# Moving each segment's four output stores from GpSimd's queue to SP's, one at each of four places in the next segment

## The chip, the cores and the metric

The kernel runs on one core of one Trainium2 chip. The core has five engines that work side by side, each through its own list of instructions in order: TensorE (PE, matrix multiplies, with the loading of weights shown apart as PEld), VectorE (DVE), ScalarE (ACT), GpSimd (POOL) and SyncE (SP), which does nothing but issue transfers. Transfers between the DRAM and the on-chip memory run on 16 DMA engines; SP, ScalarE and GpSimd can issue them. The metric is the time of one execution on the device in microseconds (us), lower being better.

## The reference

The function has two independent parts, whose results stand side by side in the last dimension of the output (1 x 2048 x 1280). Part A is a dilated sliding-window attention of 32 heads. Part B is the one that matters here: a recurrent attention with a small memory. It walks through the 2048 rows of x in 64 segments of 32 rows, and each segment needs the memory that the segment before it has made:

```python
mem = mem0                                     # 8 x 640
for s in range(64):
    xs = x[:, s * 32:(s + 1) * 32, :]
    h = jnp.concatenate([mem, xs], axis=1)     # 40 rows
    q = jnp.einsum('btd,dhe->bhte', h, Wq)     # 32 heads of 192
    k = jnp.einsum('btd,dhe->bhte', h, Wk)
    v = jnp.einsum('btd,dhe->bhte', h, Wv)
    scores = jnp.einsum('bhqe,bhke->bhqk', q, k) * scale
    scores = jnp.where(mask[None, None], scores, -1000000000.0)
    p = _softmax(scores, axis=-1)
    o = jnp.einsum('bhqk,bhke->bhqe', p, v)
    o = jnp.einsum('bhte,hed->btd', o, Wo)
    mem = o[:, :8, :]                          # memory of the next segment
    outs.append(o[:, 8:, :])                   # 32 rows of the output
```

Wq, Wk and Wv are 640 x 6144 each and Wo is 6144 x 640, all in bf16: together more than the on-chip memory holds.

## The kernel before

Part A runs first. Part B begins while it ends, some 150 us into the execution, and goes on to the end.

**Weights.** They are cut into units: a unit of q, k or v is 128 x 1536 elements (384 KB), named by its matrix, its head group g (four groups of eight heads) and one of five slices of the 640 inputs; a unit of o is 128 x 1280 (320 KB), 24 of them. Most units lie in the on-chip memory throughout (tiles named wres_q, wres_k, wres_v, wres_o). The others are streamed: in every segment 8 units of k, 10 of v and 5 of o are read again from copies in the DRAM (wcopy_k, wcopy_v, wcopy_o). All units of q are resident. Streamed units land in a pool of seven buffers (tiles named t). `get_unit(u)` gives the resident tile or calls `fetch(u)`, whose L474 issues the transfer on SP. Such a transfer has to wait until TensorE has finished with the unit that stood in the same buffer, seven fetches earlier.

**One segment.** Its work is a list of tokens, written out by hand in `ORDER` (`FIRST` for segment 0), and `step` carries out one token after another. For each head group g: `q.g`, `k.g`, `v.g` project (L561 in `project32`), `e.` tokens copy the results out (ScalarE or VectorE, L567 and L600), `T.` tokens transpose them in VectorE (L571), `S.g` makes the scores (L625), `sb`, `mx`, `sub`, `send` are the softmax, `tp`, `PT` and `mix` apply it to the values (L664, L688), `ot` keeps the result (L696 to L698). `out.g.h` projects the first three groups' results by Wo (L713), `last` the fourth's (L739). `close` (L743 to L751) ends the segment: it adds the parts, writes the new memory rows into HX, from which the next segment's projections read (L747), and writes all 32 rows into the tile XS (L748). XS holds four blocks of 160 columns one under the other, 32 partitions each, and the four stores of L750 write 24 rows of each block to the output. XS is also the tile into which `load_x` (L534, at the token `ve.2`) brings the x rows of the next segment, and from which `turn_x` (L530, at the token `tx`) transposes them into HX.

TensorE takes 32 rows at a time, so a segment's own projections hold the 8 memory rows and the first 24 rows of x. The last 8 rows of x take a path of their own, since their projections need no memory: they are made for four segments together, for a different part of the head groups in every segment, kept in small tiles (Lb, L591) and copied into place by GpSimd (L586, L607). The result for these rows goes to the DRAM by way of the tile OL and the transfer late_o (L697, L698, both on GpSimd) and is projected by Wo after the last segment (`project_late`).

**What sets the order.** The instructions of TensorE, VectorE, ScalarE and SP stand in the order in which the code calls them. So a fetch stands on SP where `get_unit` is called for its unit, and SP comes to it as soon as all issues before it have gone out; SP is ahead of TensorE by up to the seven buffers. GpSimd's instructions are placed by the scheduler.

The order of the tokens around the change, of segments 1 to 63:

```python
ORDER = """
    q.0 e.q0 T.q0 k.0 k.1 e.k0 T.k0 q.1 S.0 sb.0 e.k1 e.q1 mx.0 sub.0 v.0 T.q1 ve.0 T.k1 q.2 S.1 send.0
    e.q2 T.q2 sb.1 mx.1 k.2 tp.0 v.1 e.k2 q.3 PT.0 sub.1 mix.0 T.k2 send.1 tp.1 S.2 ve.1 ot.0 sb.2 e.q3
    PT.1 mx.2 sub.2 k.3 T.q3 send.2 out.0.0 e.k3 v.2 out.0.1 mix.1 T.k3 S.3 ot.1 tp.2 sb.3 mx.3 v.3 PT.2
    ve.2 mix.2 sub.3 out.1.0 send.3 out.1.1 ot.2 tp.3 ve.3 out.2.0 out.2.1 part tx PT.3 mix.3 ot.3 last
    join ql close eql Tql
"""
```

The streamed units of a segment go out in this order: k0 (2), k1 (2), v0 (3), k2 (2), v1 (2), k3 (2), v2 (3), v3 (2), then the load of XS, then o (5).

Of the kernel before, what the change touches and what calls it, by code (L numbers as in the profile page):

```python
# [23 lines left out]
def part_a(ctx, tc, A_x, A_wqkv, A_wo, out, ident, emit_loads):  # L24
# [241 lines left out]
    with tc.manual_schedule(engines={mybir.EngineType.PE, mybir.EngineType.DVE, mybir.EngineType.Activation}):  # L266
        pq = ps_q.tile([128, BIG], FP32, tag="q")
        for _ in range(LEAD_IN):
            nc.tensor.matmul(pq[:, 0:8], lhsT=ident, rhs=ident[:, 0:8], start=True, stop=True)
# [35 lines left out]
EVACUATE = {"k0": "SV", "k1": "SS", "k2": "VS", "k3": "SS", "q0": "VV", "q1": "SS", "q2": "SS", "q3": "VV"}  # L305
HEADS = ("VS", "SV", "VS", "SV")
SPREAD = "SSVV"
LEAD_IN = 114
HEAD = 10

# [8 lines left out]
def part_b(ctx, tc, B_x, B_mem0, B_Wq, B_Wk, B_Wv, B_Wo, out, ident, n_seg, pre, nbuf, mid):  # L319
    nc = tc.nc  # L320
    Dm, H, Dh, M, SEG, L = 640, 32, 192, 8, 32, 40
# [3 lines left out]
    out2 = out.rearrange("b s d -> (b s) d")  # L325
# [203 lines left out]
    def turn32(dst, src):  # L529
        nc.vector.transpose(dst, src.rearrange("p (f k) -> p k f", k=5))  # L530
# [39 lines left out]
    def turn_in_place(t):  # L570
        nc.vector.transpose(t, t)  # L571

    def columns_of(m, n0, n1):
        t = KT[:] if m == "k" else QT[:, 0:12 * L].rearrange("p (f n) -> p f n", n=L)
        return t[:, :, n0:n1]
# [19 lines left out]
    def project_qk(s, m, g):  # L595
        return project32([ahead, main] if renewed(s, m, g) else [main], m, g)

    def evacuate(m, ps, copies):
        sb = to_sb(ps[0], copies[0]) if len(ps) > 1 else None
        copies[1](columns_of(m, 0, 32), ps[-1][:].rearrange("p (f n) -> p f n", n=32))  # L600
        return sb

    def fill_late(s, m, g, sb):
        if sb is not None:
            return turn_late(sb, m, g, s, s)
        b = late.pop((m, g, s))
        nc.gpsimd.tensor_copy(columns_of(m, 32, L), b[:])  # L607
        free.append(b)

    def values(s, g):  # L610
        return project32([ahead, main] if renewed(s, "v", g) else [main], "v", g)

    def keep_values(g, ps):
        S_(Vst[:], ps[-1][:])  # L614
        if len(ps) > 1:
            S_(LV[g][:], ps[0][:])

    def scores(g):
        Sps = bank()[:, 0:4 * L].rearrange("p (a n) -> p a n", n=L)
        for outer in range(2):  # L620
            for a in range(4):
                for h in range(2):
                    k0, k1, c = (0, 128, 2 * h) if outer else (64 * h, 64 * h + 64, 1)
                    f = 3 * a + c
                    nc.tensor.matmul(Sps[64 * h:64 * h + 64, a, :], lhsT=QT[k0:k1, L * f:L * f + 64], rhs=KT[k0:k1, f, :],  # L625
                                     start=(outer == 0 and a == 0), stop=(outer == 1 and a == 3),
                                     tile_position=(k0, 64 * h))
        return Sps

    def soft_begin(Sps):  # L630
        nc.vector.scalar_tensor_tensor(out=Sps, in0=Sps, scalar=scale,  # L631
                                       in1=mask[:].unsqueeze(1).to_broadcast([128, 4, L]),
                                       op0=ALU.mult, op1=ALU.add)
        return Sps

    def soft_max(t1):
        mx = small.tile([128, 4], FP32, tag="mx")
        nc.vector.tensor_reduce(out=mx[:], in_=t1[:], axis=AX.X, op=ALU.max)  # L638
        return mx

    def soft_exp(t1, mx):
        nc.vector.tensor_tensor(t1[:], t1[:], mx[:].unsqueeze(2).to_broadcast([128, 4, L]), op=ALU.subtract)
        nc.scalar.activation(t1[:], t1[:], ACTF.Exp)

    def soft_end(s, g, t1):
        sm = small.tile([128, 4], FP32, tag="mx")
        nc.vector.tensor_reduce(out=sm[:], in_=t1[:], axis=AX.X, op=ALU.add)
        nc.vector.reciprocal(sm[:], sm[:])
        put_p(s, g, t1, sm)
# [18 lines left out]
    def spread_p(g, pt):  # L668
        PT = one.tile([128, 4, 2, L], BF16, tag="PT")
        if SPREAD[g] == "S":  # L670
            for b in range(2):
# [71 lines left out]
    def close(s, Y, part, partT):  # L743
        Ysb, T = XS[:], Vst[:, 0:320].bitcast(FP32).rearrange("p (k n) -> p k n", n=SEG)
        if s + 1 < n_seg:
            turn32(T, Y)
            nc.vector.tensor_tensor(HX[:, 0, :, 0:M], T[:, :, 0:M], partT[:, :, 0:M], op=ALU.add)  # L747
        nc.vector.tensor_tensor(Ysb, Y, part, op=ALU.add)  # L748
        for j in range(4):
            nc.gpsimd.dma_start(out2[SEG * s:SEG * s + SEG - M, Dm + 160 * j:Dm + 160 * j + 160],  # L750
                                Ysb[32 * j + M:32 * j + SEG])  # L751

    def segment(s):
        last = s + 1 == n_seg
        engine = {"S": S_, "V": V_}
        got = {}

        def project(m, g):
            if m == "v":
                got["v", g] = values(s, g)  # L760
            else:
                got[m, g] = project_qk(s, m, g)
                if last and (m, g) == ("k", 3):
                    load_late((2, 3))

        def step(name, *at):
            g = int(at[0][-1]) if at else None
            if name in "qkv":
                project(name, g)
            elif name == "e":  # L770
                m = at[0][0]
                got["sb", m, g] = evacuate(m, got.pop((m, g)), [engine[c] for c in EVACUATE[at[0]]])
            elif name == "T":
                m = at[0][0]
                keep = fill_late(s, m, g, got.pop(("sb", m, g)))
                turn_in_place(columns_of(m, 0, 32))
                if m + at[0][1] == "k0" and s and keep:
                    got["keep"] = keep
                elif keep:
                    keep()  # L780
                if at[0] == "k1" and "keep" in got:
                    got.pop("keep")()
            elif name == "S":
                got["S", g] = scores(g)
            elif name == "sb":
                got["t", g] = soft_begin(got.pop(("S", g)))
            elif name == "mx":
                got["mx", g] = soft_max(got["t", g])
            elif name == "sub":
                soft_exp(got["t", g], got.pop(("mx", g)))  # L790
            elif name == "send":
                soft_end(s, g, got.pop(("t", g)))
            elif name == "tp":
                got["p", g] = turn_p(g)
            elif name == "PT":
                got["PT", g] = spread_p(g, got.pop(("p", g)))
            elif name == "ve":
                keep_values(g, got.pop(("v", g)))
                if g == 2:
                    load_x(s + 1)  # L800
                elif last and g == 1:
                    load_late((0, 1))
            elif name == "mix":
                got["mix", g] = mix(g, got.pop(("PT", g)))
            elif name == "ot":
                keep_mix(s, g, got.pop(("mix", g)), [engine[c] for c in HEADS[g]])
            elif name == "out":
                g, half = int(at[0]), int(at[1])
                if "Y" not in got:
                    got["Y"] = ps_y.tile([128, 320], FP32, tag="y", name="Y")  # L810
                project_out(got["Y"], g, range(4 * half, 4 + 2 * half))
            elif name == "part":
                got["part"] = join_begin(got["Y"])
            elif name == "join":
                join_end(got["Y"], got["part"])
                got["partT"] = None if last else turn_part(got["part"])
            elif name == "tx":
                turn_x(s + 1)
            elif name == "ql":
                got["ql"] = None if last else project32([ahead], "q", (s + 1) % 4)  # L820
            elif name == "eql":
                got["sbl"] = None if last else to_sb(got["ql"][0], S_)
            elif name == "last":
                got["Z"] = bank()[:, 0:160]
                project_last(got["Z"])
            elif name == "close":
                close(s, got["Z"], got["part"], got["partT"])
            elif name == "Tql":
                if not last:
                    gl = (s + 1) % 4  # L830
                    turn_late(got["sbl"], "q", gl, s, s + 1)()

        for token in (ORDER if s else FIRST).split():
            step(*token.split("."))
# [3 lines left out]
    def load_late(quads):  # L838
        for b in quads:
            nc.sync.dma_start(res[DEAD[b]], late_o[b].rearrange("p g i c -> p (g i c)"))  # L840
# [143 lines left out]
```

## Time and profile before

| | us |
|---|---|
| median of 3 runs (lowest, highest) | 1881.22 (1872.94, 1895.54) |
| the profiled execution | 1883.37 |
| its span | 1881.6 |

The granted clock of TensorE in the profiled execution was 0.987 of full speed. The transfers that matter, as the page lists them (line, engine, count, size of each, median time from issue to landing):

| transfer | issued by | count | KB each | us to landing |
|---|---|---|---|---|
| t<-wcopy_v (L474) | SP | 640 | 384.0 | 5.9 |
| t<-wcopy_k (L474) | SP | 512 | 384.0 | 5.5 |
| t<-wcopy_o (L474) | SP | 330 | 320.0 | 5.3 |
| late_o<-OL (L698) | GpSimd | 256 | 24.0 | 5.1 |
| out_dram<-XS (L750) | GpSimd | 256 | 7.5 | 4.7 |
| XS<-xwindows (L534) | SP | 64 | 40.0 | 1.9 |

How to read the profile: a row of the timeline has the start, the time taken, the engine, the line, the operation, what is written and read, and how many instructions were merged into it (x3); in brackets stands how long the engine was idle before it, and what released it. A row of the waits has who waited, for whom, then the total in us, the number of times and the longest. SP's rows (SPq) are issues: they take 0.32 us, and the transfer goes on after them. All times are counted from the start of the span.

### The profile page before, as it was taken

Reading aid. Unit: us, or ns where it says so; the run is one execution under the profiler, and the core shown is the slowest. Engines: PE = TensorE matmul, PEld = TensorE weight load, DVE = VectorE, ACT = ScalarE, POOL = GpSimd, SP = SyncE. Lnnn points to the kernel's source line nnn. Section 1 sums busy time; section 2 is a strip of 40 time slices with the busy share of each in tenths; the row PEclk is TensorE's granted clock in tenths of the full one; section 3 lists DMA queues with packets and bytes.
Section 4 is the critical chain, followed back from the end, with each engine's and each line's share of the span. In section 5 each row is a group of like instructions: output and inputs, shape, how many; then the busy total and the mean of one; then the engine's idle time right before and its main releaser. Section 6 shows DMA issues by size and latency. Waiting matters only on the chain.

```text
span 1881.6 us, 91589 instructions
## 1 busy us (share of the span) xinstructions
PE 1646.5 (88%) x39286; PEld 1043.9 (55%) x39286; DVE 1289.3 (69%) x3671; ACT 682.5 (36%) x1821; POOL 680.5 (36%) x1876
## 2 busy tenths in 40 slices
PE   8998898888888888888888888888889888888887
PEld 5565555555555555555555555555555555555567
DVE  4886677777777777676777777776777777677730
ACT  3454333333333333333333333333333333333310
POOL 3001333344434343433434443433443333444321
PEclk9999999999999999999999999998999999999999
DMA  9926999999999999999999999998999999999991
GB/s 327 317 73 231 388 357 348 360 356 355 348 354 355 355 353 352 340 363 315 361 352 349 363 356 357 372 337 309 369 372 351 360 352 356 333 365 351 348 355 30
DMA packets 276851, 627.64 MB, mean 334 GB/s; under 512 B 60084, under 2 KB 75890, under 8 KB 276444
## 3 DMA queue, kind: packets, MB, share of 16 engines
q1 hardware_dynamic: 257596, 608.42, 90.4%
q0 software_dynamic: 18784, 13.32, 2.3%
q8 instruction: 308, 5.05, 1.1%
q14 instruction: 99, 0.81, 0.1%
q10 hardware_dynamic: 64, 0.04, 0.0%
HBM read 607.47 MB, written 22.91 MB: 335 GB/s over the span
## 4 chain that ended last, share of the span: by engine, by line
PE 54%; DVE 14%; DMA 14%; issue 7%; POOL 6%; ACT 4%; SPq 0%; ACTq 0%; POOLq 0%; DVEq 0%
PE acc L561 27%; DMA t<-wcopy_v 7%; PE Y L713 6%; PE px L625 5%; PE px L688 4%; PE pq L95 3%; DMA late_o<-OL 3%; PE px L739 3%; POOL out_dram L750 2%; DMA t<-wcopy_k 2%; PE px L664 2%; PE px L856 1%; DVE mx L638 1%; DVE px L631 1%; DVE prod L151 1%
## 5 line engine op out<-in xcount | busy, mean ns | idle before, releaser
L561 PEld LDWEIGHTS <-HX 128*32 128x32 bf16 x19380 | 502.3, 97 | 360.2 <-issue 127.0
L561 PE MATMUL acc<-t,HX 128*32 128x384 bf16 x5812 | 435.7, 331 | 32.1 <-DMA t<-wcopy_v 12.6
L561 PE MATMUL acc<-wres_q,HX 128*32 128x384 bf16 x6460 | 326.4, 332 | 22.8 <-issue 11.4
L561 PE MATMUL acc<-wres_k,HX 128*32 128x384 bf16 x3876 | 274.6, 330 | 15.7 <-issue 13.8
L697 POOL COPY OL<-OT 128x96 bf16<-128x96 bf16 x256 | 158.9, 621 | 257.2 <-ACT OT L696 147.8
L561 PE MATMUL acc<-wres_v,HX 128*32 128x384 bf16 x3232 | 215.8, 330 | 2.6 <-issue 2.2
L607 POOL COPY QT<-Lb 128x96 bf16<-128x96 bf16 x252 | 66.7, 265 | 407.0 <-PE px L625 407.0
L696 DVE CAST OT<-px 128x240 bf16<-128x240 f32 x256 | 103.3, 404 | 143.8 <-PE px L688 136.1
L713 PE MATMUL Y<-wres_o,OT 128*32 128x320 bf16 x3840 | 192.7, 302 | 8.6 <-issue 8.3
L625 PE MATMUL px<-KT,QT 64*64 64x40 bf16 (+1 forms) x4096 | 139.3, 189 | 49.6 <-DVE KT L571 23.9
L571 DVE STREAM_TRANSPOSE QT<-QT 128x384 bf16<-128x384 bf16 x256 | 146.6, 573 | 42.2 <-ACT QT L600 40.1
L600 ACT CAST KT<-acc 128x384 bf16<-128x384 f32 x192 | 92.3, 481 | 225.2 <-PE px L625 173.9
L625 PEld LDWEIGHTS <-QT 64*64 64x64 bf16 (+1 forms) x4096 | 108.3, 109 | 111.2 <-issue 46.9
L631 DVE SCALAR_TENSOR_TENSOR px<-px,mask 128x160 f32<-128x160 f32 x256 | 82.7, 323 | 124.0 <-PE px L625 123.7
L698 POOL DMA_DIRECT2D late_o<-OL x256 | 139.4, 545 | 77.9 <-POOL OL L697 60.2
L614 ACT CAST Vst<-acc 128x384 bf16<-128x384 f32 x256 | 123.6, 483 | 110.6 <-PE px L688 87.3
L696 ACT CAST OT<-px 128x240 bf16<-128x240 f32 x256 | 92.4, 361 | 190.0 <-PE px L688 110.7
L567 ACT CAST sb<-acc 128x384 bf16<-128x384 f32 x115 | 55.0, 478 | 262.2 <-PE acc L561 180.5
L713 PEld LDWEIGHTS <-OT 128*32 128x32 bf16 x4608 | 115.1, 97 | 60.7 <-issue 14.4
L571 DVE STREAM_TRANSPOSE KT<-KT 128x384 bf16<-128x384 bf16 x256 | 142.2, 556 | 2.8 <-ACT KT L600 1.2
L750 POOL DMA_DIRECT2D out_dram<-XS x256 | 129.2, 511 | 9.7 <-issue 4.0
L688 PE MATMUL px<-PT,Vst 64*128 64x80 bf16 (+1 forms) x2048 | 123.2, 212 | 9.2 <-issue 6.1
(103 smaller groups left out, 2507.2 us busy)
## 6 DMA issues: line engine op xcount, KB each, us to landing
t<-wcopy_v SPq DMA_DIRECT2D x640, 384.0 KB, 5.9
t<-wcopy_k SPq DMA_DIRECT2D x512, 384.0 KB, 5.5
t<-wcopy_o SPq DMA_DIRECT2D x330, 320.0 KB, 5.3
wres_q<-in_B_Wq_dram SPq DMA_DIRECT2D x20, 384.0 KB, 7.8
late_o<-OL POOLq DMA_DIRECT2D x256, 24.0 KB, 5.1
wres_q<-late_o SPq DMA_DIRECT2D x16, 384.0 KB, 7.3
wres_o<-in_B_Wo_dram SPq DMA_DIRECT2D x19, 320.0 KB, 7.1
wres_k<-in_B_Wk_dram SPq DMA_DIRECT2D x12, 384.0 KB, 7.9
```

Of the source, the lines that this page charges most:

```text
L561: nc.tensor.matmul(ps[n][32 * j:32 * j + 32].rearrange("p (f n) -> p f n", n=32), lhsT=X[:, dc, :], rhs=columns(w, (m, g, dc), j), start=( ...
L571: nc.vector.transpose(t, t)
L600: copies[1](columns_of(m, 0, 32), ps[-1][:].rearrange("p (f n) -> p f n", n=32))
L614: S_(Vst[:], ps[-1][:])
L625: nc.tensor.matmul(Sps[64 * h:64 * h + 64, a, :], lhsT=QT[k0:k1, L * f:L * f + 64], rhs=KT[k0:k1, f, :], start=(outer == 0 and a == 0), st ...
L631: nc.vector.scalar_tensor_tensor(out=Sps, in0=Sps, scalar=scale, in1=mask[:].unsqueeze(1).to_broadcast([128, 4, L]), op0=ALU.mult, op1=ALU ...
L688: nc.tensor.matmul(ps[r][lo:hi, 2 * L * k:2 * L * k + 2 * L], lhsT=V[64 * r:64 * r + 64, col:col + hi - lo], rhs=PT[64 * r:64 * r + 64, 2 ...
L696: copy(OT[:, 6 * r:6 * r + 6].rearrange("p c n -> p (c n)"), ps[r][:, 0:6 * L])
L697: nc.gpsimd.tensor_copy(OL[:, g % 2].rearrange("p n c -> p c n"), OT[:, :, 32:L])
L698: nc.gpsimd.dma_start(late_o[s // 4][:, g, s % 4], OL[:, g % 2].rearrange("p n c -> p (n c)"))
L713: nc.tensor.matmul(Y[t:t + 32].rearrange("p (b c) -> p b c", b=2), lhsT=OT[:, slot(c), 0:32], rhs=quarter(w, ("o", i, 0), 2 * r + gv), sta ...
L750: nc.gpsimd.dma_start(out2[SEG * s:SEG * s + SEG - M, Dm + 160 * j:Dm + 160 * j + 160], Ysb[32 * j + M:32 * j + SEG])
```

## The change

The four stores at the end of `close` are no longer issued there on GpSimd. They are put into a list, and in the next segment `step` issues one of them on SP ahead of each of the four tokens named in `STORE_AT`; by `ORDER` these come as v.0, q.2, k.2, S.2. The last segment, which has none after it, issues its four on GpSimd as before. The store's data and destination are the same.

```diff
+STORE_AT = ("q.2", "v.0", "k.2", "S.2")
...
         nc.vector.tensor_tensor(Ysb, Y, part, op=ALU.add)
-        for j in range(4):
-            nc.gpsimd.dma_start(out2[SEG * s:SEG * s + SEG - M, Dm + 160 * j:Dm + 160 * j + 160],
-                                Ysb[32 * j + M:32 * j + SEG])
+        stores.extend((out2[SEG * s:SEG * s + SEG - M, Dm + 160 * j:Dm + 160 * j + 160], Ysb[32 * j + M:32 * j + SEG])
+                      for j in range(4))
+        if s + 1 == n_seg:
+            while stores:
+                nc.gpsimd.dma_start(*stores.pop(0))
+
+    stores = []
...
         def step(name, *at):
             g = int(at[0][-1]) if at else None
+            if ".".join((name,) + at) in STORE_AT and stores:
+                nc.sync.dma_start(*stores.pop(0))
             if name in "qkv":
                 project(name, g)
```

## The prediction

> **What bounds the kernel now.** I read the head of the page first, then the share of the DMA engines by stretch, then the timeline of SP's issues against VectorE's close of a segment, then the waits.
>
> ```profile
> span 1881.6 us, 91589 instructions
> PE 1646.5 (88%) x39286; PEld 1043.9 (55%) x39286; DVE 1289.3 (69%) x3671; ACT 682.5 (36%) x1821; POOL 680.5 (36%) x1876
> ...
> PE 54%; DVE 14%; DMA 14%; issue 7%; POOL 6%; ACT 4%; SPq 0%; ACTq 0%; POOLq 0%; DVEq 0%
> ```
>
> TensorE leads by busy time, and the chain that ended last goes through it most, but no engine is full. The busy shares by stretch show what is (the last two figures of a row are the share of the 16 DMA engines and the GB/s):
>
> ```profile
> core 0: us, PE busy (x) PEld busy (x) DVE busy (x) ACT busy (x) POOL busy (x), PEclk, DMA share, GB/s
> 300.00:1780.00 1480.00, 1298.07 (x32326) 807.05 (x32318) 1053.81 (x3207) 540.03 (x1496) 583.96 (x1625) 0.99 0.98 352
> 1006.00:1012.00 6.00, 5.55 (x133) 3.23 (x126) 4.94 (x18) 3.38 (x11) 0.66 (x3) 1.00 1.01 383
> ...
> 1024.00:1027.00 3.00, 2.71 (x67) 1.86 (x71) 1.91 (x6) 0.48 (x1) 2.63 (x6) 1.00 1.04 406
> ```
>
> Over the whole of part B the DMA engines are 98% busy: the weight stream has almost no idle time to give. Single stretches reach 383 and 406 GB/s against the mean of 352, so some of a delay can be made up, but not at will. The stream runs well because SP issues far ahead of TensorE. One segment's issues, with the end of the segment before it:
>
> ```profile
> 1005.04 0.80 SPq L474 DMA_DIRECT2D t<-wcopy_k  x2
> 1005.93 4.15 SPq L474 DMA_DIRECT2D t<-wcopy_v  x5
> 1010.26 0.32 SPq L534 DMA_DIRECT2D XS<-xwindows  x1
> 1012.16 5.14 SPq L474 DMA_DIRECT2D t<-wcopy_o  x5
> ...
> 1017.87 3.35 SPq L474 DMA_DIRECT2D t<-wcopy_k  x4
> 1021.58 3.33 SPq L474 DMA_DIRECT2D t<-wcopy_v  x3
> 1026.60 1.65 SPq L474 DMA_DIRECT2D t<-wcopy_k  x2
> ...
> 1025.15 0.33 DVE L748 TENSOR_TENSOR XS<-px,QT 128x160 bf16<-128x160 f32 x1
> ```
>
> The four k units and the three v units of the next segment's first groups are asked for before L748 closes the present one, at 1025.15 + 0.33 = 1025.48. The first v unit goes out 3.9 us before that, the third (it starts 0.32 us before the end of its row, at 1024.59) 0.9 us before.
>
> **The change part by part.** In the order of the changed program the four stores stand on SP: one ahead of the first v unit (the token v.0), two together ahead of k.2's first unit (q.2 asks for no streamed unit), one ahead of k3's. All 63 segments after the first carry the stores of the segment before. So the first store waits for L748, and behind it on SP stand all later fetches: the three v units can no longer go out before the close. That is the added wait. Those that wait for it are TensorE's matmuls L561 on these units, and the DMA engines, which get nothing new meanwhile. The same place in two other segments:
>
> ```profile
> 509.52 2.85 SPq L474 DMA_DIRECT2D t<-wcopy_v  x3
> ...
> 512.18 0.33 DVE L748 TENSOR_TENSOR XS<-px,QT 128x160 bf16<-128x160 f32 x1
> ...
> 1504.00 2.77 SPq L474 DMA_DIRECT2D t<-wcopy_v  x3
> ...
> 1506.66 0.33 DVE L748 TENSOR_TENSOR XS<-px,QT 128x160 bf16<-128x160 f32 x1
> ```
>
> After the change the first v unit goes out one issue step behind the close; a step is about 0.4 us (two issues in 0.80 us at 1005.04). Delay of that unit: 512.51 + 0.4 - 509.52 = 3.4 us; 1025.48 + 0.4 - 1021.58 = 4.3 us; 1506.99 + 0.4 - 1504.00 = 3.4 us. What covers it is the queue that stands ahead of it:
>
> ```profile
> L474 SPq DMA_DIRECT2D t<-wcopy_v x580: 319/320/2002, 307.9 to 1774.1; - x194
> ...
>   PE acc L561: 10.1, 23
> ...
> DMA to landing us min/median/max: 3.1/5.9/7.6
> ```
>
> A v unit usually lands 5.9 us after its issue and at best 3.1 us after it, so 5.9 - 3.1 = 2.8 us of a usual landing is time behind other transfers. A later issue costs nothing until that is used up; then the DMA engines run dry: by 3.4 - 2.8 = 0.6, 4.3 - 2.8 = 1.5 and 0.6 us here. The middle of the three is 0.6, their mean 0.9; I take 0.75 us in each of 63 segments: 47 us. Bounds: 63 x 0 = 0, if queues are longer where the delay is longer, and 63 x 1.5 = 95 us.
>
> By the Trainium skill, "DMA: Bandwidth & Descriptors", section "Anatomy of one DMA — SWDGE (gpsimd) path", a lone DMA takes about 2.0 us plus its bytes at 436 GB/s, which for 384 KB is an estimate of 2.9 us; the fastest landing here is 3.1. By that figure the cover would be 3.0 us and this term 63 x 0.55 = 35 us instead of 47.
>
> How TensorE feels it, in the segment after 1025.48:
>
> ```profile
> 1029.45 0.54 PE L625 MATMUL px<-KT,QT 64*64 64x40 bf16 x16
> 1029.91 0.51 PE L561 MATMUL acc<-t,HX 128*32 128x384 bf16 x8
> 1030.25 0.50 PE L561 MATMUL acc<-wres_v,HX 128*32 128x384 bf16 x8
> 1030.60 0.35 PE L561 MATMUL acc<-t,HX 128*32 128x384 bf16 x4
> ...
> 1032.63 0.54 PE L625 MATMUL px<-KT,QT 64*64 64x40 bf16 x16 [0.87 <-DVE KT L571]
> ```
>
> The third v unit, begun at 1030.60, was issued at 1024.59. Delayed, the first issues at 1025.9 and lands at 1025.9 + 3.1 = 1029.0, and each of the two behind it one transfer later, 384 KB at 352 GB/s = 1.1 us: the third lands at 1031.2, 0.6 us after TensorE wants it. Behind it TensorE then stood idle 0.87 us for VectorE's transpose, which swallows such a delay. This is the first give-back:
>
> ```profile
> PE px L625 <- DVE KT L571: 23.9, 40, 0.9
> PE px L625 <- POOL QT L607: 13.4, 15, 3.1
> ...
> PE px L625 <- POOL Lb L591: 1.9, 11, 0.2
> ```
>
> 23.9 us in all stand in such waits, and not all behind v.0; I take half, -12 us (bounds -24 and 0).
>
> GpSimd loses four issues a segment:
>
> ```profile
> L750 POOL DMA_DIRECT2D out_dram<-XS x256 | 129.2, 511 | 9.7 <-issue 4.0
> ...
> 1025.77 2.02 POOL L750 DMA_DIRECT2D out_dram<-XS  x4
> 1027.78 0.88 POOL L591 COPY Lb<-sb 128x96 bf16<-128x96 bf16 x4
> 1028.62 0.26 POOL L607 COPY QT<-Lb 128x96 bf16<-128x96 bf16 x1
> ```
>
> That is 252 x 0.511 = 129 us of GpSimd's time, and it brings the copies of L591 and L607 up to 2.0 us forward; the scores of head group 0 (L625) need them. TensorE's matmuls waited for GpSimd there 13.4 + 1.9 = 15 us in all. But the scores come just ahead of v.0, whose data are now tied to the close: arriving earlier mostly means waiting longer for them. I take -5 us (bounds -15 and 0).
>
> The rest costs nothing. SP is idle for far longer than four issue steps (from 1010.58 to 1012.16, for one). The bytes of the stores, 252 x 7.5 KB, were moved before as well. The reload of XS (L534) must await the last store, issued ahead of k3's units; there that is 1005.0, with a usual landing by 1010.9, against the reload's 1010.26: 0.6 us late at worst and the next issue on SP came only at 1012.16.
>
> Sum: 47 - 12 - 5 = +30 us on the profiled execution's 1883.4 us (span 1881.6, about 1.8 us around it): 1913. The median of the runs, 1881.2, is 2 us lower than that execution, which makes 1911.
>
> **The rivals.** Faster: the cover holds and GpSimd's time counts. The chain that ended last runs, in some segments, right through the stores:
>
> ```profile
> 975.71 2.02 POOL out_dram L750 x4
> 977.73 0.87 POOL Lb L591 x4
> 978.60 0.22 POOL QT L607
> ...
> 978.86 0.56 PE px L625 x16
> ```
>
> The page puts L750 at 2% of that chain, 38 us, or 19 segments of 2.0 us. For it: TensorE waited for v units in 23 of the 580 issues only, 10.1 us. Against it: the 0.98 above, and an issue that falls behind the close in every segment looked at. It decides if the queue ahead of the first v unit is regularly longer than 3.4 us rather than 2.8. Half of the 38 us, since the chain closes up behind them: 1881 - 19 = 1862. Chance 0.14.
>
> No change: the cover is just enough, and what GpSimd gives pays the remainder; the terms at their near ends are 0.25 x 63 - 12 - 5 = -1 us, so 1880. Chance 0.20.
>
> Slower in full: nothing is made up, since an engine at 98% has no spare time; 95 us, 1976. By the Trainium skill, "DMA: Bandwidth & Descriptors", section "Specifications", reads from the memory are limited to about 358 GB/s for a core, by which the mean of 352 would leave 2% for catching up and this case would be likely. The stretches of 383 and 406 GB/s disagree with so flat a limit, so it gets 0.10.
>
> Slower by the queue's own order: SP's DMAs take eight completion semaphores in turn, and each waits for the landing of the one eight places before:
>
> ```profile
> SPq L474 <- PE px L739: 86.3, 115, 2.5
> ...
> SPq L474 <- DMA t<-wcopy_v: 12.6, 35, 1.6
> ```
>
> The first of these rows says that 115 fetches, about two a segment, go out when the last projection (L739) frees a buffer, just ahead of the close that reads that projection. The second is a wait for a landing, small today. With three stores among eight DMAs a fetch may wait for the fifth weight before it instead of the seventh: if that costs half a transfer, 0.55 us, per segment on top, 30 + 63 x 0.55 = 65 us, 1946. Chance 0.08.
>
> **How the numbers follow.** Forecast 0.48, rivals 0.14, 0.20, 0.10 and 0.08. The forecast's own range goes from 1893 (a segment's loss of 0.45 us in place of 0.75) to 1935 (1.1 us). The range that leaves out the full bubble and the lower half of the faster case, under 2 in 10, is 1868 to 1955. About 1% (19 us) is what a measurement here can tell from no change. Faster by that (under 1862): most of the first rival, which is spread to both sides of its 1862 and further below, 0.11. Within: the second rival, the rest of the first and the forecast's low edge, 0.20 + 0.03 + 0.04 = 0.27. Slower: 0.62.
>
> **What would show it.** SP's row for the first v unit should start behind L748 instead of 3 to 4 us ahead of it, with its three issues 0.4 us apart; the landing of v units should have a median nearer to 4 us; the DMA share of 300 to 1780 us should drop to about 0.96; TensorE's waits for wcopy_v should grow from 10.1 us in that stretch to 30 or more, and its waits for L607 go. GpSimd's L591 should start right behind its L607. The prediction is wrong if the DMA share stays at 0.98 with the first v unit issued late, or if the first v unit is found to stand behind more than 3.4 us of other transfers.

## The result, and the profile after

| | us |
|---|---|
| before, median of 6 runs (lowest, highest) | 1888.11 (1872.94, 1895.54) |
| after, median of 6 runs (lowest, highest) | 1943.04 (1935.56, 1947.87) |
| ratio of after to before, 95% interval | 1.0294 (1.0261 to 1.0327) |
| span of the profiled execution, before and after | 1881.6 and 1946.1 |

The change makes the kernel 55 us slower by the medians. The three runs that were known at the time of the prediction had a median of 1881.2; three more, made beside the changed kernel, raise it to 1888.1. In the changed kernel all lines behind the new constant are one higher, and those behind `close` some more: L562 is the projection, L626 the scores, L749 the close's write of XS, L774 the new store on SP.

The head of the page of the changed kernel and the chain that ended last, by engine and by line:

```profile
span 1946.1 us, 91372 instructions
...
PE 48%; DMA 34%; DVE 9%; ACT 4%; issue 4%; SPq 1%; POOL 0%; ACTq 0%; DVEq 0%; POOLq 0%
PE acc L562 25%; DMA t<-wcopy_v 23%; DMA t<-wcopy_k 9%; PE Y L714 6%; PE px L689 3%; PE px L740 3%; PE pq L95 3%; PE px L626 3%; PE px L863 1%; DVE OT L697 1%; ACT OT L697 1%; ACT QT L721 1%; DVE prod L151 1%; PE po L161 1%; PE px L665 1%
```

Transfers, 14% of the chain before, are 34% now, and GpSimd's 6% are gone. So both halves of the change did what they were expected to do: the chain no longer runs through GpSimd's issues, and now runs through the v units.

The timeline of the changed kernel around one close, SP's issues and VectorE's L749:

```profile
1019.10 3.35 SPq L475 DMA_DIRECT2D t<-wcopy_k  x4
1025.75 0.33 SPq L774 DMA_DIRECT2D out_dram<-XS  x1
1026.18 1.29 SPq L475 DMA_DIRECT2D t<-wcopy_v  x3
1027.52 0.82 SPq L774 DMA_DIRECT2D out_dram<-XS  x2
1028.44 0.84 SPq L475 DMA_DIRECT2D t<-wcopy_k  x2
...
1025.41 0.32 DVE L749 TENSOR_TENSOR XS<-px,QT 128x160 bf16<-128x160 f32 x1
```

SP's last k unit goes out by 1022.45; then SP stands still until L749 ends at 1025.73, issues the store, and only then the three v units, 0.45 us behind the close where the first stood 3.9 us ahead of it before. What the DMA engines do meanwhile is seen in stretches of 2 us around that close (the last two figures are their share and the GB/s), in the changed kernel:

```profile
300.00:1780.00 1480.00, 1280.29 (x31208) 787.31 (x31204) 1019.62 (x3100) 521.84 (x1447) 451.97 (x1346) 0.98 0.94 340
1022.70:1024.70 2.00, 1.37 (x72) 1.19 (x72) 1.29 (x4) 0.93 (x3) 0.54 (x1) 1.00 1.02 363
1024.70:1026.70 2.00, 2.00 (x61) 1.12 (x53) 1.39 (x5) 0.48 (x1) 1.17 (x2) 1.00 0.49 184
1026.70:1028.70 2.00, 2.00 (x56) 1.54 (x50) 1.49 (x4) 0.48 (x1) 1.10 (x5) 1.00 0.72 199
1028.70:1030.70 2.00, 1.94 (x51) 1.38 (x42) 1.27 (x4) 0.13 (x2) 0.58 (x3) 1.00 1.03 393
```

and in the kernel before, around its close at 1025.48:

```profile
1024.50:1026.50 2.00, 2.00 (x55) 1.33 (x48) 1.44 (x5) 0.48 (x1) 1.71 (x5) 1.00 1.01 403
1026.50:1028.50 2.00, 2.00 (x56) 1.37 (x48) 1.93 (x4) 0.00 (x0) 2.00 (x7) 1.00 0.97 311
```

Over the four microseconds that follow 1 us ahead of the close, 184 and 199 GB/s stand against 403 and 311: (403 + 311 - 184 - 199) x 2 us = 662 KB, which at 340 GB/s are 1.9 us of transfer lost in this segment. By the share, the engines were idle for 2 x (0.51 + 0.28) = 1.6 us of these four. This segment is a usual one: the same count around all 63 closes gives 1.5 us in the mean (0.6 to 2.7), against 0.0 in the kernel before. Over part B the share of the engines fell from 0.98 to 0.94. The segments make up a part of it: the span grew by 64.5 us, 1.0 us for each of 63 segments.

The waits of the changed kernel, SP's own first, then TensorE's (us in total, how many, the longest):

```profile
SPq L774 <- DVE XS L749: 216.5, 63, 4.8
...
SPq L475 <- DMA t<-wcopy_v: 77.7, 132, 2.7
```

```profile
PE acc L562 <- DMA t<-wcopy_v: 105.5, 166, 3.4
...
PE acc L562 <- DMA t<-wcopy_k: 29.2, 55, 3.0
...
PE px L626 <- DVE KT L572: 1.7, 4, 0.7
...
PE px L626 <- POOL QT L608: 0.8, 1, 0.8
```

The first of SP's rows is the added wait itself: 63 times, 3.4 us each. In the kernel before, TensorE's waits for the same units were these:

```profile
PE acc L561 <- DMA t<-wcopy_v: 12.6, 28, 1.3
PE acc L561 <- DMA t<-wcopy_k: 5.0, 14, 0.7
```

From 17.6 us they rose to 134.7 us together, 117 more. Told apart by the unit waited for, 78 us of them are for v.0's three units (1.4 before) and 23 us for k.2's two (1.1 before), which stand right behind them on SP. Against that, its waits for the transposes (23.9 before) and for GpSimd (13.4) are all but gone.

### The profile page after: what moved, and what is told of

Read it like the earlier page. It is cut to its first block, busy times and chain, and to the rows that moved or that the text cites. A ratio compares the mean times of both kernels' runs of the same rounds, so it can differ in the third digit from the quotient of the medians.

```text
span 1946.1 us, 91372 instructions
## 1 busy us (share of the span) xinstructions
PE 1677.7 (86%) x39286; PEld 1054.0 (54%) x39286; DVE 1290.3 (66%) x3671; ACT 681.6 (35%) x1821; POOL 554.0 (28%) x1624
## 4 chain that ended last, share of the span: by engine, by line
PE 48%; DMA 34%; DVE 9%; ACT 4%; issue 4%; SPq 1%; POOL 0%; ACTq 0%; DVEq 0%; POOLq 0%
PE acc L562 25%; DMA t<-wcopy_v 23%; DMA t<-wcopy_k 9%; PE Y L714 6%; PE px L689 3%; PE px L740 3%; PE pq L95 3%; PE px L626 3%; PE px L863 1%; DVE OT L697 1%; ACT OT L697 1%; ACT QT L721 1%; DVE prod L151 1%; PE po L161 1%; PE px L665 1%
## 5 line engine op out<-in xcount | busy, mean ns | idle before, releaser
L562 PEld LDWEIGHTS <-HX 128*32 128x32 bf16 x19380 | 514.0, 98 | 469.9 <-issue 224.9
L562 PE MATMUL acc<-t,HX 128*32 128x384 bf16 x5812 | 448.3, 336 | 144.6 <-DMA t<-wcopy_v 105.5
L562 PE MATMUL acc<-wres_q,HX 128*32 128x384 bf16 x6460 | 332.3, 337 | 8.3 <-issue 6.6
L562 PE MATMUL acc<-wres_k,HX 128*32 128x384 bf16 x3876 | 273.0, 333 | 5.7 <-issue 4.2
L562 PE MATMUL acc<-wres_v,HX 128*32 128x384 bf16 x3232 | 217.5, 335 | 0.6 <-issue 0.5
L714 PE MATMUL Y<-wres_o,OT 128*32 128x320 bf16 x3840 | 187.8, 301 | 1.7 <-issue 1.7
L626 PE MATMUL px<-KT,QT 64*64 64x40 bf16 (+1 forms) x4096 | 141.2, 191 | 9.8 <-issue 5.9
L626 PEld LDWEIGHTS <-QT 64*64 64x64 bf16 (+1 forms) x4096 | 109.7, 111 | 71.1 <-issue 44.9
L644 ACT ACTIVATE px<-px 128x160 f32<-128x160 f32 x256 | 75.2, 294 | 140.1 <-DVE px L643 135.5
```

The costliest lines, as they stand in the source:

```text
L562: nc.tensor.matmul(ps[n][32 * j:32 * j + 32].rearrange("p (f n) -> p f n", n=32), lhsT=X[:, dc, :], rhs=columns(w, (m, g, dc), j), start=( ...
L714: nc.tensor.matmul(Y[t:t + 32].rearrange("p (b c) -> p b c", b=2), lhsT=OT[:, slot(c), 0:32], rhs=quarter(w, ("o", i, 0), 2 * r + gv), sta ...
```

## The experiments

The theory after the first reading: the first store's wait for the close, with three fetches behind it on SP, is the whole loss. The main rival was that SP is the wrong place for four more transfers wherever they stand, by its queue or by its eight completion semaphores. Each kernel is compared with runs of the kernel before on the same chip, whose median was 1888.5 us for the first four, 1887.2 for the next four and 1883.5 for the last three. Unless something else is shown, the diffs are against the changed kernel.

**No store ahead of v.0.**

```diff
-STORE_AT = ("q.2", "v.0", "k.2", "S.2")
+STORE_AT = ("q.2", "k.2", "S.2", "k.3")
```

> All four stores stay on SP, but none stands ahead of v.0 any more: two stand together ahead of the first unit of k2 and two ahead of the first unit of k3, when the close is over. Theory W (the first store's wait for the close holds back the three fetches of v.0, and this alone makes the change slower): the 55 us go, and GpSimd's four issues stay away, so 1865 to 1888 us. Rival Q (the loss comes from four more transfers on SP, in its queue of weights and in the turn of its eight completion semaphores): still 1925 us or more.

Measured: 1880.5 us, ratio 0.9970 (0.9938 to 1.0002). The 55 us are gone with all four stores still on SP, and the time is no different from before, perhaps a little better. SP's waits in this kernel:

```profile
SPq L475 <- DMA t<-wcopy_v: 64.6, 121, 2.4
SPq L774 <- DMA t<-wcopy_v: 45.4, 75, 2.0
...
SPq L774 <- DVE XS L749: 28.4, 57, 0.7
```

The store still waits for the close, but 0.5 us at a time, and with no fetch of v.0 behind it. The waits for landings, which come with the turn of the semaphores, are larger for v units than in the changed kernel (64.6 + 45.4 = 110 against 77.7 + 20.8 = 98 us, with the stores' own), and cost little.

**One store alone ahead of v.0**, the other three at the close on GpSimd as before.

```diff
-STORE_AT = ("q.2", "v.0", "k.2", "S.2")
+STORE_AT = ("v.0",)
...
             while stores:
                 nc.gpsimd.dma_start(*stores.pop(0))
+        else:
+            for _ in range(3):
+                nc.gpsimd.dma_start(*stores.pop())
```

> One store alone goes from SP, ahead of v.0; the other three go from GpSimd at the close, as before. W: the wait is there in full, so 1930 to 1955 us, a little over the changed kernel if GpSimd's time counts. Q: a quarter of the loss, about 1902 us.

Measured: 1943.9 us, ratio 1.0296 (1.0235 to 1.0357): the whole loss with a quarter of the stores. It is the wait, not what is transferred. That GpSimd issues three of four here and the time is still that of the changed kernel says that GpSimd's time is worth nothing that these runs can tell as long as v.0 waits for its data; the interval reaches some 11 us to either side.

**The same wait, with fewer fetches behind it.** The first store is issued inside `fetch`, ahead of one unit chosen by name: the second of v.0 as in the diff, the third in the next kernel, ("v", 0, 4), and the first of k.1 in the one after, ("k", 1, 1). The other stores stay at q.2, k.2 and S.2.

```diff
+HOLD = ("v", 0, 1)
...
     def fetch(u):
+        if u == HOLD and stores:
+            nc.sync.dma_start(*stores.pop(0))
         t = wstream.tile([128, SLOT], BF16, tag="ws")
```

> The first store stands one fetch later than in the changed kernel: the first unit of v.0 goes out early, the second and third wait for the close. The second unit's issue moves by about 2.1 us (from 1.5 us ahead of the close to 0.5 behind it). If the queue covers 2.8 us, as the prediction had it, there is no loss: 1888 us or less. If it covers 1.9 us (usual landing 5.9 us less the 4.0 us that the fastest landing takes in the changed kernel), about 0.2 us a segment are lost and partly made up: 1880 to 1900 us. Q: 1925 us or more.

> The first store stands two fetches later: only the third unit of v.0 waits for the close, and moves by about 1.5 us. W: within either cover, so no loss, the same as e1 within 10 us. Q: 1925 us or more.

Measured: with the second and third unit held 1921.4 us, ratio 1.0184 (1.0137 to 1.0231), a miss of both covers; with the third alone 1892.9 us, ratio 1.0039 (1.0005 to 1.0073), which is 12 us over the kernel that holds none (its stores stand two and two) and so just outside the 10 us that were allowed. How far the second unit is moved follows from where it stood in the kernel before, in the three segments of the prediction, whose closes ended at 512.51, 1025.48 and 1506.99:

```profile
511.05 1.31 SPq L474 DMA_DIRECT2D t<-wcopy_v  x2
```

```profile
1023.11 0.32 SPq L474 DMA_DIRECT2D t<-wcopy_v  x1
```

```profile
1505.54 1.23 SPq L474 DMA_DIRECT2D t<-wcopy_v  x2
```

If it goes out 0.45 us behind the close, as the first unit did above, it is moved by 1.9, 2.8 and 1.9 us, within the 2.8 us that the prediction took for free; and the pair still costs 1921.4 - 1880.5 = 41 us against none held. TensorE's waits in this kernel show where:

```profile
PE acc L565 <- DMA t<-wcopy_v: 46.5, 99, 1.9
PE acc L565 <- DMA t<-wcopy_k: 40.7, 52, 3.1
```

Only 12.5 us of these are for v.0's units, the held ones among them; 39 us are for k.2's, which do not wait for the close and stand behind them on SP (2 us with none held). The DMA engines were idle for 0.8 us of the four around a close in the mean, for 0.2 us with the third unit alone held, and for 0.0 with none. So a delay within the 2.8 us was not free: the held units themselves came almost in time, but the engines ran dry meanwhile, and the units behind came late.

**More fetches behind it.** With the wait ahead of the first unit of k.1 five units are held.

> The first store stands two fetches earlier than in the changed kernel, ahead of the first unit of k.1: five units wait for the close instead of three. W: the DMA engines run dry two transfers (2.2 us) sooner. One, two and three held units cost 12, 41 and 63 us against the kernel that holds none (1880), some 20 to 30 us for each further unit, so about 100 to 125 us: 1980 to 2005 us. Rival (SP's wait for the close costs as such, whatever stands behind it): 1943 us, as the changed kernel.

Measured: 2084.7 us, ratio 1.1062 (1.0981 to 1.1143). The rival is out, but the forecast is missed too: 204 us over none held, twice the straight line. TensorE's waits show why, in the rows of this kernel:

```profile
PE acc L565 <- DMA t<-wcopy_k: 186.2, 145, 3.8
...
PE acc L565 <- DMA t<-wcopy_v: 35.1, 83, 1.4
```

By `ORDER` it comes to k.1 right behind k.0, and to v.0 only behind the scores of group 0. So it has little other work while the stream restarts: the first row alone, 5.0 us in the kernel before, is 186 us, beside 204 us of added time.

**No stores at all.**

```diff
-        stores.extend((out2[SEG * s:SEG * s + SEG - M, Dm + 160 * j:Dm + 160 * j + 160], Ysb[32 * j + M:32 * j + SEG])
+        list((out2[SEG * s:SEG * s + SEG - M, Dm + 160 * j:Dm + 160 * j + 160], Ysb[32 * j + M:32 * j + SEG])
                       for j in range(4))
```

> The stores of segments 0 to 62 are left out altogether, so 24 of each segment's 32 rows of part B are not written. It shows what four issues at a segment's start cost on GpSimd, with nothing put on another queue. If GpSimd's 2.0 us a segment are worth the 5 us of the prediction: 1875 to 1888 us. If they are worth the 38 us that the chain showed: 1850 us. If it is faster than the kernel with all stores behind v.0 (1880) by more than 8 us, the stores cost something on SP too.

Measured: 1871.2 us, ratio 0.9926 (0.9896 to 0.9955): 16 us less than before by the medians, between the two forecasts. So the four stores at the start of a segment, issues and transfers together, were worth about 16 us, where no fetch was held. It is 9 us faster than the kernel with two and two stores behind v.0, so these cost something on SP as well.

**All four together at q.2.**

```diff
-STORE_AT = ("q.2", "v.0", "k.2", "S.2")
+STORE_AT = ("q.2",)
...
-            if ".".join((name,) + at) in STORE_AT and stores:
+            while ".".join((name,) + at) in STORE_AT and stores:
```

> All four stores go from SP together at q.2, ahead of the first unit of k2, behind v.0's three. W: no fetch is held for the close, so 1872 to 1890 us, as with two and two. If the turn of the eight semaphores costs (four stores in a row among eight transfers, so that later fetches wait for the landing of v.0's units): 1895 to 1915 us.

Measured: 1891.7 us, ratio 1.0034 (0.9997 to 1.0071), between the two forecasts. SP's waits in it:

```profile
SPq L475 <- DMA t<-wcopy_v: 121.9, 247, 2.0
```

247 fetches wait for the landing of a v unit, where 35 did before. In the built program SP's transfers take eight completion semaphores in turn; a row of four stores uses up half of them, and the fetches behind must wait for the landing of units that went out just ahead. That is the queue's own price, and it is some 20 us at most (against the kernel without stores), not 55.

**The stores on ScalarE's queue**, at the close, in the kernel before.

```diff
-            nc.gpsimd.dma_start(out2[SEG * s:SEG * s + SEG - M, Dm + 160 * j:Dm + 160 * j + 160],
+            nc.scalar.dma_start(out2[SEG * s:SEG * s + SEG - M, Dm + 160 * j:Dm + 160 * j + 160],
```

> The kernel before, with the four stores issued at the close by ScalarE in place of GpSimd: no store on SP, so no fetch waits. W: no loss from fetches; ScalarE's copies at the start of the next segment are up to 1.6 us later (four issues of about 0.4 us), of which ScalarE's idle time takes most: 1875 to 1900 us. Rival (any queue but GpSimd's makes it slower): 1925 us or more.

Measured: 1932.1 us, ratio 1.0247 (1.0182 to 1.0311), against the forecast and within the rival's, though the kernels with SP's stores behind v.0 contradict that rival's reason, that any queue but GpSimd's is slower. The waits of this kernel that grew, ScalarE's behind its stores, then TensorE's, then SP's, and last TensorE's for ScalarE in the kernel before:

```profile
ACT sb L567 <- DMA out_dram<-XS: 106.2, 25, 6.9
```

```profile
PE px L625 <- DVE KT L571: 48.0, 79, 0.9
PE acc L561 <- ACT sb L567: 43.5, 50, 2.3
```

```profile
SPq L474 <- DMA t<-wcopy_k: 145.1, 76, 3.6
...
SPq L474 <- DMA out_dram<-XS: 17.5, 26, 1.8
```

```profile
PE acc L561 <- ACT sb L567: 10.7, 11, 2.6
```

TensorE waited 10.7 us for ScalarE's sb before, and 43.5 now; its waits for KT have doubled. In the built program ScalarE's and SP's transfers take their turn on the same eight semaphores. In that turn the four stores stand between v.0's units and k.2's, just as in the kernel with all four at q.2, so that SP's fetch for k.2 must wait for the landing of a k.1 unit. That kernel is 20 us over the one without stores, and this one 61 us. So the turn explains about a third at most, if it costs the same here; the rest is put down to ScalarE's copies behind the stores by the rows alone.

**Spare matmuls in the wait.** TensorE's granted clock fell with the change: the mean over its runs is 0.977, and 0.986 in the kernel with no store ahead of v.0. To see whether that is a cost of its own, 16 matmuls whose result is not used were put into v.0, once into the changed kernel and once, as a price list, into the kernel with no store ahead of v.0.

```diff
         for dc in range(5)[part]:
...
+            if (m, g) == ("v", 0) and dc < 2:
+                spare = ps_y.tile([128, 320], FP32, tag="y", name="spare") if dc == 0 else spare
+                for j in range(8):
+                    nc.tensor.matmul(spare[32 * (j % 4):32 * (j % 4) + 32], lhsT=main[:, 2, :], rhs=res["v", 0, 2][:, 0:320],
+                                     start=True, stop=True, tile_position=(0, 32 * (j % 4)))
```

> The changed kernel with 16 spare matmuls in every v.0 (8 behind the first streamed unit's, 8 behind the second's; their result is not used), about 1.3 us of work at the full clock where TensorE waits for the held units. In the changed kernel TensorE's granted clock was at half in 24 stretches of 3.4 us in part B, against 11 before, and its mean fell from 0.987 to 0.974. If that fall costs about 20 of the 55 us and comes from the waits at v.0: the clock returns to 0.985 or more and the time falls to 1920 to 1935 us. If the clock's fall costs nothing of its own: 1943 us or more, up to 1975 if the spare work is not free.

> The same 16 spare matmuls in the kernel whose four stores all stand behind v.0 (1880 us without them), to price them where TensorE does not wait. 63 x 1.3 us = 82 us of work on TensorE, of which the idle time ahead of S.1 takes a part: 1900 to 1950 us. If they are free even here: 1880 us.

Measured: 1953.1 us, ratio 1.0355 (1.0316 to 1.0394); without the wait 1903.0 us, ratio 1.0109 (1.0074 to 1.0145). The mean clock of the four runs is 0.985 in both, so the spare work brought back most of what the clock had lost. At this equal clock the wait still costs 1953.1 - 1903.0 = 50 of the 62.5 us between the two kernels without spare work (1943.0 - 1880.5). So the fall of the clock is at most a side effect, worth some 12 us by these medians, and even these may be spare work that the wait hides; the two are not told apart by these runs.

**One store at a time, all behind v.0.**

```diff
-STORE_AT = ("q.2", "v.0", "k.2", "S.2")
+STORE_AT = ("k.2", "v.1", "k.3", "v.2")
```

> All four stores on SP, one each ahead of k.2, v.1, k.3 and v.2, so that no two stand together and none ahead of v.0's units. W: no fetch is held for the close: 1870 to 1885 us, as with two and two (1880) or a little faster, since no more than one store lies between a fetch and the landing that it must await in the turn of the eight semaphores. If the reload of XS then waits for the last store, which goes out later: up to 1900 us.

Measured: 1871.2 us, ratio 0.9932 (0.9905 to 0.9959). This version beats both kernels, the one before by 12 us or 0.7%, and is as fast as the kernel that leaves the stores out. The share of the DMA engines in it, over the same stretch as above, and SP's waits:

```profile
300.00:1780.00 1480.00, 1313.72 (x32756) 820.25 (x32760) 1068.66 (x3256) 547.66 (x1518) 475.01 (x1413) 0.99 0.99 357
```

```profile
SPq L475 <- DMA t<-wcopy_v: 69.0, 132, 1.7
SPq L535 <- DMA out_dram<-XS: 50.9, 51, 2.0
SPq L774 <- DVE XS L749: 32.4, 59, 0.8
```

The reload of XS now waits 1.0 us for the last store in 51 segments, and the time does not show it. The engines move 357 GB/s against 352 before and 340 after the change.

## Why the prediction was right or wrong

**The mechanism was right.** The first store's wait, SP's standing still until the close, the three v units behind it, the share of the engines falling and TensorE waiting for wcopy_v came as forecast; the fall of the share, to 0.94, was deeper than the 0.96 named. The runs with one store alone and with no store ahead of v.0 show that this wait is all of the loss.

**The size was not**, and the term that failed is the time for which the DMA engines run dry: the delay less the cover. The prediction let the queue hide 2.8 us, the usual landing of 5.9 us less the fastest of 3.1, and was left with 0.75 us a segment, 47 us. Measured, the engines were idle for 1.5 us of the four around a close, about 92 us in 63 segments, twice the term. The delay of the first unit was near the forecast: issued 0.45 us behind the close it is 3.6 us, in the mean over the segments of the kernel before. So it was the cover that was too large, some 2.1 us in place of 2.8, and in it the restart of a dry queue, which the prediction took to be as quick as the fastest landing: the first unit 3.1 us after its issue, the others 1.1 us apart, the third 5.3 us after the first issue. TensorE's timeline in the changed kernel, behind the close at 1025.73, tells otherwise:

```profile
1030.46 0.35 PE L562 MATMUL acc<-t,HX 128*32 128x384 bf16 x4
1032.05 0.34 PE L562 MATMUL acc<-t,HX 128*32 128x384 bf16 x4 [1.24 <-DMA t<-wcopy_v]
1032.21 0.51 PE L562 MATMUL acc<-wres_v,HX 128*32 128x384 bf16 x8
1033.01 0.51 PE L562 MATMUL acc<-t,HX 128*32 128x384 bf16 x4 [0.29 <-DMA t<-wcopy_v]
```

TensorE was ready for the second v unit at 1030.81 and got it at 1032.05; the third came at 1033.01. From the first issue at 1026.18 that is 6.8 us to the third landing instead of 5.3, and the third is there 7.3 us behind the close where the prediction had 5.7. The trace tells the landing of the third unit in 31 segments: the median is 6.3 us after the first issue, the least 5.3. So the prediction's restart is the best case and not the usual one. It is the same with the first unit in the kernel with five units held, whose landing the trace tells in 31 segments: 3.1 us after its issue at the least, 3.7 us in the median. With 3.7 in place of 3.1 the cover is 5.9 - 3.7 = 2.2 us, and 3.6 - 2.2 = 1.4 us are left, near the 1.5 measured. One thing stays open: where the second unit was the first held, moved by 2.0 us in the mean, this cover should have been enough, and the engines were still idle for 0.8 us.

The sign that was named for it, a median landing near 4 us, did not come, as the view over part B in the changed kernel shows:

```profile
DMA to landing us min/median/max: 4.0/6.0/8.1
```

But this row was no good sign: the trace tells only the landings of one unit of v.0, the third, and one of v.2, and none of the first unit behind the close. The Trainium skill, "DMA: Bandwidth & Descriptors", section "Anatomy of one DMA — SWDGE (gpsimd) path", gives 2.0 us plus the bytes at 436 GB/s, measured there on GpSimd's path and not on SP's, by which a lone 384 KB transfer takes an estimated 2.9 us; the first unit behind a dry queue took 3.7 us in the median here, so the figure would have made the forecast worse: 35 us for this term in place of 47.

The prediction also followed the loss no further than the third v unit. The runs show it at the units behind as well: k.2's cost TensorE 23 us in the changed kernel, and more than v.0's where only the second and third were held.

**Term by term.** The wait less what is made up was put at 47 - 12 = 35 us; it is 1943.0 - 1880.5 = 62.5 us between the changed kernel and the one with no store ahead of v.0. The rest, GpSimd's relief and the stores' own place on SP, was put at -5 us; it is 1880.5 - 1888.5 = -8 us, made of about -16 for the relief and +8 for the stores in pairs. The give-back by the transposes, -12, was if anything too small, since 22 of the 23.9 us went. So the term of 47 us carries the miss: 62.5 + 22 = 85 us would be wanted in its place, near the 92 us of idle time. The split depends on the order in which the two are taken: with the wait in place, the run with one store says that GpSimd's relief is worth about nothing, and the wait some 55 us. The fall of TensorE's clock was not in the sum at all; by the runs with spare matmuls it is worth some 12 us at most.

**The rivals.** The full bubble at 95 us was right about the hole, 92 us, and wrong about the time: with 62.5 us lost, about a third was made up, as in the forecast's structure; in the segment shown the engines reach 393 GB/s right behind the hole. The semaphores' turn is real, but costs nothing that shows with single stores, 8 us in pairs and 20 us with four in a row, and not on top of the wait: with one store instead of four the time is the same. The faster case failed at the point named for it: the queue ahead of the first v unit is not longer than its delay. Its other half was sound, and shows up where the wait is away: 16 us.

## What to carry to other kernels

A queue that runs ahead of the compute engines is worth what it runs ahead; a small transfer that waits for a late result, put into that queue, takes all of the lead away, however small it is. Put it behind the last fetch that may go out before the result is there, and one at a time rather than in a row if completion semaphores are taken in turn. And price a restart of the stream by the usual landing of units that meet an empty queue, not by the fastest landing of all, and look for the loss at the units behind the held ones too.

## What the runs showed of the hardware

TensorE's granted clock fell as more units were held: 0.986 in the mean of the runs with no unit held, 0.987 with one, 0.982 with two, 0.977 with three, 0.955 with five. The clock records of the traces show stretches of 3.4 us at half the clock, 22 of them in part B after the change (two twice as long) and 11 before (one twice as long). The Trainium skill, "TensorE: Matmul & The Clock Gate", section "HAM oscillation — how this bites in real kernels", describes a clock that falls to half when waits for transfers cross a window of about 3.4 us. The length of the stretches agrees; the waits do not: in the 3.4 us ahead of each such stretch of the changed kernel no idle time of TensorE was longer than 1.9 us, and in 18 of the 22 the longest was a wait for a v unit. So here waits shorter than that window went with the fall.

ScalarE's queue was no free place for four small stores: the engine was busy 35% of the span, and the kernel was still 45 us slower. The row of its waits names the stores for 106 us of its own copies' waiting.
